# Attention and mixture of experts on one core: v's sums shared by two engines, the router's weights first, the last batch in another order

## The chip, the core and the metric

The program runs on one core of a Trainium2 chip. The core has five engines that run side by side and wait for each other through semaphores: TensorE (PE: matrix products; PEld: its weight loads), VectorE (DVE), ScalarE (ACT), GpSimd (POOL) and SyncE (SP), which here mostly issues transfers. Each engine takes its instructions in order. The metric is the device time of one execution in microseconds (us), as the median of several runs.

## The reference

Eight batches, eight heads, 576 tokens, 64 numbers per head. Keys and values are first averaged over groups of eight tokens, so 576 queries meet 72 keys:

```python
k_p = k.reshape(B, H, Sp, pool, D).mean(axis=3)          # pool = 8
v_p = v.reshape(B, H, Sp, pool, D).mean(axis=3)
scores = scale * np.matmul(q, k_p.transpose(0, 1, 3, 2))
attn = softmax(scores);  x = attn @ v_p                  # x: (4608, 512)
```

Then a router in two steps (the best of 4 groups, then the best of its 4 experts) sends every token to one of 16 experts, and the token's output is its gate times `relu(x @ w1) @ w2` of that expert, with 1024 hidden numbers.

## The kernel before

**Batches.** A batch is 576 tokens: five chunks of 128, 128, 128, 128 and 64. For each batch the attention is computed, the router run, and the expert that most tokens want is applied to the whole batch. The tokens of other experts come afterwards, in blocks of 32 (class `Left`).

**Plans.** The order of the work is written out by hand as strings of pieces: `START`, then `FIRST` for batch 0, `STEADY` for batches 1 to 6, `LAST` for batch 7. A piece such as `a.vr:0:r` calls the method `vr(0, "r")` of the attention of the current batch; `n` and `x` are the attentions of the next two batches, `m` and `w` the expert's work of this batch and the next, `t` the router's weights and dummies, `l` the leftover blocks. Each engine takes its instructions in the order of the plan, transfers included: nearly all are issued by SP, a few by ACT. A transfer into a buffer still in use, or from an address that the kernel has yet to compute, holds SP and all that stands behind it.

**The opening.** `load_k`, `load_v` bring keys and values in two blocks each (512 KB); `load_r` the remainder of 16 rows per head pair: 64 lanes of v (`rem[0:64]`) and 64 of k (`rem[64:128]`). `kr`, `vr` and `rr` add groups of eight by `total` (L211): on VectorE one reduction (`r`), on Pool three additions that halve the row (`p`). `kt` (L263) turns the summed keys on TensorE, and its `tail` the keys' remainder; `kta` copies them. `qt` and `qta` turn and copy a chunk of queries. `sc`, `mx`, `sb`, `ex`, `su_`, `nm`, `pt` are the softmax of a chunk: scores (PE), maximum and subtraction (DVE), exponential (ACT), sums (DVE), normalization (POOL, `:p`), transposition (DVE). `rep` (L239) spreads the summed values to where the attention product `av` wants them; `repa` and `repd` copy them by ACT and VectorE. `ava` and `avd` take the product out.

**The guess.** Batch 0 takes its expert by a guess from the averaged values alone: `guess_x` (L476, 20 small products of all of `vp` and the remainder), one ACT copy, `guess_e` (L486, four products with the router's weights and some small VectorE operations), and SP reads the elected number in `elect` (L472). Only then can SP issue `m.load:1:j`, the expert's weights of 512 KB each. `split` (ACT) and `spd` (VectorE `v` or two Pool subtractions `p`) part each weight block into a high and a low piece. `up` (L567) is a first expert product of 12 passes: `up:f` reads weight block f//2. `ua`, `upd` take it out; `down` (8 passes a piece) and `half` are the second product. `t.load_wr` asks, on ACT's queue, for the router's weights in two transfers; `turn_wr` turns them on TensorE, `put_wr` copies them. `t.warm:z` multiplies ones by ones z times (two passes each), with a result that nobody reads.

**Last batch.** Its plan mixes the expert's work with the leftover blocks: ten `l.step`, `l.which`, fetches, then `whole`, `turn`, `gather`, `up`, `down` of one block. Before, its first product is `m.up:3:0`.

Of the kernel before, what the change touches and what calls it, by code (L numbers as in the profile page):

```python
# [8 lines left out]
F32 = mybir.dt.float32  # L9
# [8 lines left out]
B, H, S, D = 8, 8, 576, 64  # L18
# [16 lines left out]
TCARGS = dict(schedule_with_timeline_sim=True)  # L35

START = """
a.load_k:1:w a.load_k:0:w a.load_q:0 a.qt:0 a.load_r:k a.load_r:v a.load_q:1 a.kr:0:r a.kr:1:p a.load_v:0 a.load_v:1 a.rr:r a.qta:0 a.load_q:3 a.kt
n.load_r:v t.load_wr a.kta a.qt:1 a.load_q:4 a.vr:0:r a.sc:0 a.mx:0 t.turn_wr a.qta:1 a.vr:1:p a.sc:1 a.load_q:2 t.warm:2 a.sb:0 n.load_r:k a.ex:0
n.load_k:0 a.mx:1 t.put_wr a.sb:1 a.su_:0 a.qt:3 a.ex:1 a.rep a.guess_x a.nm:0:p a.su_:1 a.repd:1 a.repa:1 a.nm:1:p n.load_v:1 a.pt:0 a.repa:0 a.qt:2  # L40
a.repd:0 a.qta:3 n.load_k:1 a.pt:1 a.guess_e n.kr:0:r a.av:0:1 a.ava:0:0 a.ava:0:1 a.avd:0:1 a.ava:0:3 a.qt:4 m.load:1:1 m.load:1:2 m.load:1:3
a.ava:0:2 a.qta:2 a.sc:3 a.avd:0:3 a.avd:0:0 m.load:1:0 a.avd:0:2 n.kr:1:p a.mx:3 a.sb:3 m.split:1:1 a.ex:3 n.load_qb:3 m.spd:1:1:v n.load_qb:1 a.sc:2
a.su_:3 t.warm:4 a.nm:3:p a.qta:4 t.warm:7
"""
FIRST = """
m.split:1:3 a.mx:2 m.up:2:0 n.load_qb:2 m.split:1:2 m.ua:2:0 a.sc:4 a.sb:2 t.warm:8 m.spd:1:2:p m.up:3:0 a.pt:3 m.up:4:0 m.up:5:0 a.ex:2 a.mx:4 a.sb:4
# [26 lines left out]
w.load:2:0 x.nm:0:p w.spd:1:0:v w.load:2:1 x.repa:1 m.da:1 m.down:11 w.split:1:1 x.pt:0 m.da:3 n.gates w.load:1:2 w.spd:1:1:p n.keep_x  # L73
"""
LAST = """
m.up:3:0 m.up:2:0 m.up:3:1 m.ua:3:0 m.split:1:3 m.ua:2:0 m.up:1:0 m.up:1:1 m.split:1:2 m.upd:2:0 l.xtiles m.ua:3:1 l.step m.ua:1:0 l.step m.spd:1:2:p
m.ua:1:1 m.up:5:0 m.spd:1:3 m.up:7:0 m.upd:3:0 m.up:4:0 m.upd:3:1 m.ua:5:0 m.ua:4:0 m.load:2:2 m.load:2:3 m.upd:1:0 m.upd:1:1 m.up:0:0 m.up:2:1
m.up:5:1 m.up:6:0 m.ua:7:0 l.step l.step l.step m.ua:2:1 m.ua:0:0 m.upd:5:0 m.up:4:1 m.split:2:1 m.ua:5:1 l.step l.step l.step m.split:2:2 m.ua:6:0
m.upd:4:0 m.up:7:1 m.ua:4:1 l.step m.spd:2:1:p m.split:2:0 l.step l.tiles m.ua:7:1 m.up:0:1 m.spd:2:0:p m.upd:7:0 m.up:6:1 l.which m.upd:0:0 m.upd:2:1
l.fetch_x l.fetch_b:1 m.split:2:3 m.spd:2:3:p m.upd:5:1 m.down:0 m.upd:6:0 l.slots m.ua:6:1 m.upd:4:1 m.upd:7:1 m.spd:2:2:v m.upd:6:1 l.rows l.whole:1  # L80
m.down:1 m.down:3 l.whole:3 l.whole:0 l.whole:2 l.whole:4 l.turn:0 l.fetch_a:1 l.turn:1 l.turn:3 m.ua:0:1 m.down:4 l.turn:2 l.turn:4 l.gather m.down:5
m.upd:0:1 m.da:1 l.next_ l.back m.half:3:1 l.up m.down:6 l.hback l.fetch_a m.down:12 l.fetch_x m.down:2 l.down l.slots m.down:13 m.down:7 m.da:0
m.down:8 l.fetch_b m.da:4 m.da:2 m.half:3:0
"""


# [1 line left out]
def attn_moe(ctx: ExitStack, tc: tile.TileContext, q, k, v, wg, we, w1, w2, out):  # L88
    nc = tc.nc
# [7 lines left out]
    ident = keep.tile([128, 128], F32, name="ident")  # L97
# [10 lines left out]
    for u in range(4):  # L108
        r = slice(32 * u, 32 * u + 32)
# [37 lines left out]
    wk = ctx.enter_context(tc.tile_pool(name="wk", bufs=1))  # L147
    sm = ctx.enter_context(tc.tile_pool(name="sm", bufs=2))
    ps_m = ctx.enter_context(tc.tile_pool(name="ps_m", bufs=3, space=PSUM))
# [9 lines left out]
    class Att:  # L159
# [67 lines left out]
                s.kp = wk.tile([128, NG, D], F32, name="kp")  # L227
            s.total(s.kp[:, 2 * u:2 * u + 2], s.k[u], eng)

        def rr(s, eng="r"):  # L230
            s.rp = wk.tile([128, D], F32, name="rp")
            s.total(s.rp, s.rem, eng)

        def vr(s, u, eng="p"):
            if s.vp is None:
                s.vp = wk.tile([128, 4, D], F32, name="vp")
            s.total(s.vp[:, 2 * u:2 * u + 2, :], s.v[u], eng)

        def rep(s):  # L239

# [20 lines left out]
            tt(out=s.v5[:, o:o + 2 * w].rearrange("p (a b) d -> p a b d", a=2), in0=ps.rearrange("p a (b d) -> p a b d", d=D), in1=ms, op=ALU.mult)  # L261

        def kt(s):  # L263
            tail = lambda ps: [nc.tensor.matmul(ps[64 * a:64 * a + 64, 256:320], lhsT=s.rp[64:128], rhs=ident[64:128, 64:128], start=True, stop=True) for a in range(2)]
            ps = s.tk = ps_t.tile([128, 512], F32, name="tp")
            if s.b:
                for z in range(2):
                    nc.tensor.transpose(out=ps[:, 128 * z:128 * z + 128], in_=flat(s.kp[:, 2 * z:2 * z + 2, :]), identity=ident)
                tail(ps)
                return  # L270
            for g in range(NG):
                for y in range(2):
                    nc.tensor.matmul(ps[64 * y:64 * y + 64, 128 * g:128 * g + 128], lhsT=s.kp[:, 2 * (g % 2) + g // 2], rhs=ident, start=True, stop=True)
            ps = s.tk2 = ps_m.tile([128, 512], F32, name="mm")
            tail(ps)

        def kta(s):
            ps = s.tk
# [682 lines left out]
```

## Time and profile before

| what | value |
|---|---|
| median of 3 runs | 556.96 us (553.56 to 557.68) |
| the profiled execution | 557.65 us |
| its span | 555.9 us |
| PE busy | 529.3 us (95%) |
| DVE, POOL, ACT busy | 360.8, 275.8, 211.7 us |
| chain that ended last | PE 83%, DVE 5%, DMA 5% |

The span is the part of the execution that the trace covers. Busy time of TensorE is modelled, as matrix products overlap. The chain that ended last is followed back from the last instruction, at each step to what released it. In a timeline row the first number is the start in us from the span's start, the second how long it took, `xN` how many instructions it stands for, and brackets give the idle time of the engine before it and what ended it.

### The profile page before, as it was taken

The numbers are of one execution on the slowest core, as the hardware profiler recorded it, in microseconds if no ns is written. First come the engines' busy times: TensorE is split into PE (matmuls) and PEld (weight loads), VectorE is DVE, ScalarE is ACT, GpSimd is POOL, SyncE is SP. The second block draws the span as 40 slices with busy tenths as digits, with TensorE's granted clock in tenths as the row PEclk, the third lists the DMA queues.
The fourth block names the chain that finished last, engine by engine and source line by source line (L and its number), as shares of the span: only waits on it lengthen the run. The fifth ranks groups of instructions, "written<-read, shape, count | busy, mean of one in ns | idle before, by whom it ended". The sixth has DMA issues, their size and how long they took to land.

```text
span 555.9 us, 15235 instructions
## 1 busy us (share of the span) xinstructions
PE 529.3 (95%) x6218; PEld 471.4 (85%) x6218; DVE 360.8 (65%) x940; ACT 211.7 (38%) x402; POOL 275.8 (50%) x259
## 2 busy tenths in 40 slices
PE   3889999999999999999999999999999999999995
PEld 3789988799888998899788998899788987799874
DVE  4678898758756775767656775767657764347420
ACT  2244523445225452454325451454234451335111
POOL 3437386036924577057914686157904644175300
PEclk9999999999999999999999999999999999999998
DMA  9787561590519714591519623693518000725701
GB/s 234 157 198 179 150 126 50 170 334 30 101 42 314 192 46 78 198 284 44 104 50 339 157 64 61 241 381 71 123 62 279 33 2 27 261 102 199 275 31 62
DMA packets 115648, 81.32 MB, mean 146 GB/s; under 512 B 73562, under 2 KB 92250, under 8 KB 115192
## 3 DMA queue, kind: packets, MB, share of 16 engines
q1 hardware_dynamic: 110256, 70.92, 45.7%
q10 hardware_dynamic: 5288, 9.35, 4.5%
q8 instruction: 50, 0.82, 0.7%
q14 instruction: 22, 0.18, 0.1%
q0 software_dynamic: 32, 0.04, 0.0%
HBM read 75.01 MB, written 28.38 MB: 186 GB/s over the span
## 4 chain that ended last, share of the span: by engine, by line
PE 83%; DVE 5%; DMA 5%; ACT 2%; issue 2%; SPq 1%; POOL 1%; ACTq 0%; POOLq 0%
PE mm L578 35%; PE mm L617 26%; PE sc L374 5%; PE mm L622 4%; PE sc L320 4%; DMA sw<-in_moe_w_dram 3%; PE tp L408 1%; DMA rem<-in_k_dram 1%; DMA ht<-in_moe_w_expert_dram 1%; PE mm L597 1%; PE sc L244 1%; PE mm L910 1%; ACT w L555 1%; PE tp L374 1%; DVE pT L355 1%
## 5 line engine op out<-in xcount | busy, mean ns | idle before, releaser
L578 PE MATMUL mm<-xt,w 128*128 128x320 f32 (+1 forms) x1536 | 212.4, 298 | 2.1 <-POOL w L565 1.2
L578 PEld LDWEIGHTS mm<-xt,w 128*128 128x128 f32 x1536 | 205.6, 189 | 5.6 <-POOL w L565 1.6
L617 PE MATMUL mm<-w,ht 128*128 128x512 f32 x744 | 177.4, 393 | 0.0
L565 POOL TENSOR_TENSOR w<-sw,w 128x512 fp32r<-128x512 f32 x94 | 122.8, 1332 | 84.9 <-ACT w L555 74.5
L617 PEld LDWEIGHTS mm<-w,ht 128*128 128x128 f32 x744 | 138.0, 188 | 31.1 <-issue 2.5
L349 POOL TENSOR_TENSOR p<-p,su 128x576 f32<-128x576 f32 (+1 forms) x40 | 45.8, 1150 | 135.7 <-DVE su L344 128.5
L583 ACT ACTIVATE ht<-mm 128x320 fp32r<-128x320 f32 (+1 forms) x128 | 49.6, 408 | 110.6 <-PE mm L578 110.3
L588 DVE SCALAR_TENSOR_TENSOR ht<-mm,ht 128x256 fp32r<-128x256 f32 (+1 forms) x192 | 60.2, 344 | 41.2 <-ACT ht L583 40.1
L555 ACT CAST w<-sw 128x1024 fp32r<-128x1024 f32 x64 | 66.1, 1043 | 19.4 <-DMA sw<-in_moe_w_dram 14.9
L630 ACT ACTIVATE y<-mm,gm 128x512 f32<-128x512 f32 x31 | 21.3, 687 | 67.7 <-PE mm L617 63.5
L399 POOL TENSOR_TENSOR sw<-xt 128x640 f32<-128x640 f32 (+1 forms) x28 | 40.0, 1461 | 7.7 <-DVE xt L392 7.7
L342 DVE TENSOR_REDUCE su<-p 128x8 f32<-128x576 f32 (+1 forms) x40 | 29.7, 743 | 15.1 <-ACT p L337 15.0
L309 DVE STREAM_TRANSPOSE qT<-q 128x512 f32<-128x512 f32 x35 | 24.4, 700 | 20.7 <-PE sc L320 14.9
L218 POOL TENSOR_TENSOR kv<-kv 128x512 f32<-128x512 f32 x21 | 29.0, 1379 | 10.0 <-DMA kv<-in_v_dram 7.7
L326 DVE TENSOR_REDUCE mx<-sc 128x8 f32<-128x576 f32 (+1 forms) x40 | 29.4, 735 | 6.2 <-PE sc L320 6.2
L374 PE MATMUL sc<-pT,v 32*64 32x128 f32 (+11 forms) x1560 | 31.0, 290 | 2.0 <-issue 1.3
L355 DVE STREAM_TRANSPOSE pT<-p 128x576 f32<-128x576 f32 (+1 forms) x40 | 30.8, 769 | 3.1 <-POOL p L349 3.1
L337 ACT ACTIVATE p<-p 128x576 f32<-128x576 f32 (+1 forms) x40 | 27.4, 684 | 13.4 <-DVE p L333 9.9
L622 PE MATMUL mm<-w,ht 128*128 128x512 f32 x128 | 32.4, 396 | 0.0
L374 PEld LDWEIGHTS sc<-pT,v 32*64 32x64 f32 (+3 forms) x1560 | 27.4, 139 | 5.1 <-issue 4.0
L561 DVE TENSOR_TENSOR w<-sw,w 128x1024 fp32r<-128x1024 f32 x17 | 25.1, 1478 | 10.0 <-ACT w L555 10.0
L320 PEld LDWEIGHTS sc<-kT,qT 64*64 64x64 f32 x1264 | 24.1, 142 | 7.4 <-issue 3.0
(217 smaller groups left out, 492.4 us busy)
## 6 DMA issues: line engine op xcount, KB each, us to landing
sw<-in_moe_w_dram SPq DMA_DIRECT2D x72, 512.0 KB
xscr<-xt SPq DMA_DIRECT2D x8, 2304.0 KB
kv<-in_v_dram SPq DMA_DIRECT2D x16, 512.0 KB
q<-in_q_dram SPq DMA_DIRECT2D x112, 72.0 KB
out_dram<-y ACTq DMA_DIRECT2D x31, 256.0 KB
kv<-in_k_dram SPq DMA_DIRECT2D x14, 512.0 KB
kv<-in_moe_w_dram SPq DMA_DIRECT2D x6, 512.0 KB
pT<-xscr SPq DMA_DIRECT2D x2, 1152.0 KB
```

The costliest lines, as they stand in the source:

```text
L320: nc.tensor.matmul(ps[t:t + 64, y, SP * g:SP * g + SP], lhsT=s.qT[c][r, g, w:w + 64], rhs=k, start=True, stop=True)
L349: (nc.vector if eng == "v" else nc.gpsimd).tensor_tensor(out=pf, in0=pf, in1=bc(sf, SP), op=ALU.mult)
L355: nc.vector.transpose(out=s.pT[0:n, :, 32 * c:32 * c + 32], in_=s.p[c].rearrange("p u x s -> p (u x s)").rearrange("p (b i) -> p b i", i=3 ...
L374: nc.tensor.matmul(to[64 * x:64 * x + 64], lhsT=w, rhs=s.pT[e, k, 32 * c0:32 * c0 + n], start=(z == 0), stop=(z == 2))
L399: nc.gpsimd.tensor_tensor(out=x, in0=a, in1=b, op=ALU.add)
L555: nc.scalar.copy(out=wh, in_=raw)
L565: nc.gpsimd.tensor_tensor(out=wl[:, p], in0=raw[:, p], in1=wh[:, p].bitcast(F32), op=ALU.subtract)
L578: nc.tensor.matmul(ps[:, 0:n], lhsT=l[:, kc, fs], rhs=xt[:, r, kc, sl], start=(kc == 0 and i == 0), stop=(kc == 3 and i == 2))
L583: nc.scalar.activation(out=s.ht[f][:, o:o + n], in_=s.pu[f, hf][:, 0:n], func=AF.Relu)
L588: stt(out=ht[:, at:at + hi - lo], in0=ps[:, lo - o:hi - o], scalar=0.0, in1=ht[:, lo:hi].bitcast(F32), op0=ALU.max, op1=ALU.subtract)
L617: nc.tensor.matmul(ps, lhsT=s.ht[f][:, 640 * l + o:640 * l + o + 128], rhs=s.w[2, f // 2][r][:, f % 2, :], start=(i == 0), stop=(i == 23))
L622: nc.tensor.matmul(ps, lhsT=s.ht[f][:, 512:640], rhs=s.w[2, f // 2][r][:, f % 2, :], start=(i == 0), stop=(i == 15))
```

## The change

In the opening `vr` can sum half a block (`t` is 0 or 1), and `rr` one part of the remainder (`v` or `k`). Of each block of v VectorE sums one half and Pool the other; VectorE sums the keys' remainder, Pool v's. The turn of the keys' remainder is a piece of its own, `ktail`. On ACT `t.load_wr` is first. On SP `load_r:v` stands behind `load_q:1` and `load_v:0`, `load_q:4` ahead of `n.load_r:v`, and `n.load_k:1` behind the four `m.load`. On TensorE `turn_wr` follows the second scores, `guess_x` precedes `qt:3` and `rep`, `qt:2` follows `guess_e`; of the dummies two stand at the start and one ahead of `guess_x`, and the two pieces at the end of `START` are 4 and 4 where they were 4 and 7. `LAST` has the same pieces in another order. `FIRST` and `STEADY` are as they were.

```diff
@@ -35,12 +35,12 @@
 START = """
-a.load_k:1:w a.load_k:0:w a.load_q:0 a.qt:0 a.load_r:k a.load_r:v a.load_q:1 a.kr:0:r a.kr:1:p a.load_v:0 a.load_v:1 a.rr:r a.qta:0 a.load_q:3 a.kt
-n.load_r:v t.load_wr a.kta a.qt:1 a.load_q:4 a.vr:0:r a.sc:0 a.mx:0 t.turn_wr a.qta:1 a.vr:1:p a.sc:1 a.load_q:2 t.warm:2 a.sb:0 n.load_r:k a.ex:0
-n.load_k:0 a.mx:1 t.put_wr a.sb:1 a.su_:0 a.qt:3 a.ex:1 a.rep a.guess_x a.nm:0:p a.su_:1 a.repd:1 a.repa:1 a.nm:1:p n.load_v:1 a.pt:0 a.repa:0 a.qt:2
-a.repd:0 a.qta:3 n.load_k:1 a.pt:1 a.guess_e n.kr:0:r a.av:0:1 a.ava:0:0 a.ava:0:1 a.avd:0:1 a.ava:0:3 a.qt:4 m.load:1:1 m.load:1:2 m.load:1:3
-a.ava:0:2 a.qta:2 a.sc:3 a.avd:0:3 a.avd:0:0 m.load:1:0 a.avd:0:2 n.kr:1:p a.mx:3 a.sb:3 m.split:1:1 a.ex:3 n.load_qb:3 m.spd:1:1:v n.load_qb:1 a.sc:2
-a.su_:3 t.warm:4 a.nm:3:p a.qta:4 t.warm:7
+t.load_wr t.warm:2 a.load_k:1:w a.load_k:0:w a.load_q:0 a.load_r:k a.load_q:1 a.qt:0 a.kr:0:r a.kr:1:p a.load_v:0 a.load_r:v a.load_v:1 a.qta:0
+a.load_q:3 a.kt a.rr:r:k a.ktail a.kta a.qt:1 a.load_q:4 a.vr:0:r:0 a.vr:0:p:1 a.rr:p:v n.load_r:v a.qta:1 a.sc:0 a.mx:0 a.sc:1 a.sb:0 t.turn_wr
+a.vr:1:r:0 a.vr:1:p:1 a.ex:0 a.mx:1 a.load_q:2 t.put_wr n.load_r:k n.load_k:0 a.sb:1 a.ex:1 t.warm:1 a.guess_x a.su_:0 n.load_v:1 a.nm:0:p a.su_:1
+a.qt:3 a.rep a.nm:1:p a.repd:1 a.pt:0 a.guess_e a.repa:1 a.repa:0 a.repd:0 a.qta:3 a.qt:2 m.load:1:1 m.load:1:2 m.load:1:3 m.load:1:0 a.pt:1
+n.load_k:1 n.kr:0:r a.av:0:1 a.qt:4 a.ava:0:0 a.ava:0:1 a.avd:0:1 a.ava:0:3 a.ava:0:2 a.qta:2 a.avd:0:3 a.avd:0:0 a.avd:0:2 a.sc:3 n.kr:1:p
+m.split:1:1 m.spd:1:1:v a.mx:3 a.sb:3 a.ex:3 n.load_qb:3 n.load_qb:1 a.sc:2 a.su_:3 t.warm:4 a.nm:3:p a.qta:4 t.warm:4
 """
...
 LAST = """
-m.up:3:0 m.up:2:0 m.up:3:1 m.ua:3:0 m.split:1:3 m.ua:2:0 m.up:1:0 m.up:1:1 m.split:1:2 m.upd:2:0 l.xtiles m.ua:3:1 l.step m.ua:1:0 l.step m.spd:1:2:p
-m.ua:1:1 m.up:5:0 m.spd:1:3 m.up:7:0 m.upd:3:0 m.up:4:0 m.upd:3:1 m.ua:5:0 m.ua:4:0 m.load:2:2 m.load:2:3 m.upd:1:0 m.upd:1:1 m.up:0:0 m.up:2:1
-m.up:5:1 m.up:6:0 m.ua:7:0 l.step l.step l.step m.ua:2:1 m.ua:0:0 m.upd:5:0 m.up:4:1 m.split:2:1 m.ua:5:1 l.step l.step l.step m.split:2:2 m.ua:6:0
...
+m.up:0:0 m.up:1:0 m.up:3:0 m.ua:0:0 m.up:3:1 l.xtiles m.ua:3:0 m.up:2:0 m.split:1:2 m.upd:0:0 l.step m.spd:1:2:p m.ua:2:0 m.ua:1:0 l.step m.up:0:1
+m.up:5:0 m.load:2:2 m.up:1:1 m.upd:3:0 m.upd:2:0 m.ua:3:1 m.upd:1:0 m.upd:3:1 l.step m.up:4:0 l.step m.up:2:1 m.ua:0:1 l.step m.upd:0:1 l.step
+m.split:1:3 m.ua:5:0 m.upd:5:0 m.split:2:1 m.ua:1:1 m.load:2:3 l.step l.step m.upd:1:1 l.step l.step m.spd:1:3 l.tiles m.ua:4:0 m.up:5:1 m.up:7:0
+l.which m.ua:2:1 m.ua:5:1 m.split:2:2 l.fetch_x m.up:6:0 m.upd:4:0 l.fetch_b:1 m.split:2:0 m.ua:6:0 m.up:4:1 m.upd:2:1 m.up:6:1 m.spd:2:0:p l.slots
+m.upd:5:1 m.ua:7:0 m.ua:4:1 m.ua:6:1 m.upd:7:0 m.upd:4:1 m.upd:6:0 m.split:2:3 m.spd:2:1:p m.upd:6:1 l.rows m.spd:2:2:v l.whole:1 l.whole:3 m.down:3
+l.whole:0 l.whole:2 m.up:7:1 l.whole:4 m.down:4 m.ua:7:1 l.turn:0 l.fetch_a:1 l.turn:1 l.turn:3 m.down:12 m.spd:2:3:p l.turn:2 l.turn:4 l.gather
+m.upd:7:1 l.next_ m.half:3:1 m.down:13 l.back m.da:4 m.down:0 l.up m.down:1 l.hback l.fetch_a m.down:2 l.fetch_x m.down:5 l.down m.down:6 m.down:7
+l.slots m.da:1 l.fetch_b m.da:0 m.down:8 m.da:2 m.half:3:0
 """
...
@@ -227,14 +227,19 @@
                 s.kp = wk.tile([128, NG, D], F32, name="kp")
             s.total(s.kp[:, 2 * u:2 * u + 2], s.k[u], eng)
 
-        def rr(s, eng="r"):
-            s.rp = wk.tile([128, D], F32, name="rp")
-            s.total(s.rp, s.rem, eng)
-
-        def vr(s, u, eng="p"):
+        def rr(s, eng="r", part=None):
+            if s.rp is None:
+                s.rp = wk.tile([128, D], F32, name="rp")
+            r = {None: slice(0, 128), "v": slice(0, 64), "k": slice(64, 128)}[part]
+            s.total(s.rp[r], s.rem[r], eng)
+
+        def vr(s, u, eng="p", t=None):
             if s.vp is None:
                 s.vp = wk.tile([128, 4, D], F32, name="vp")
-            s.total(s.vp[:, 2 * u:2 * u + 2, :], s.v[u], eng)
+            if t is None:
+                s.total(s.vp[:, 2 * u:2 * u + 2, :], s.v[u], eng)
+            else:
+                s.total(s.vp[:, 2 * u + t, :], s.v[u][:, t], eng)
 
         def rep(s):
 
@@ -261,18 +266,21 @@
             tt(out=s.v5[:, o:o + 2 * w].rearrange("p (a b) d -> p a b d", a=2), in0=ps.rearrange("p a (b d) -> p a b d", d=D), in1=ms, op=ALU.mult)
 
         def kt(s):
-            tail = lambda ps: [nc.tensor.matmul(ps[64 * a:64 * a + 64, 256:320], lhsT=s.rp[64:128], rhs=ident[64:128, 64:128], start=True, stop=True) for a in range(2)]
             ps = s.tk = ps_t.tile([128, 512], F32, name="tp")
             if s.b:
                 for z in range(2):
                     nc.tensor.transpose(out=ps[:, 128 * z:128 * z + 128], in_=flat(s.kp[:, 2 * z:2 * z + 2, :]), identity=ident)
-                tail(ps)
+                s.ktail(ps)
                 return
             for g in range(NG):
                 for y in range(2):
                     nc.tensor.matmul(ps[64 * y:64 * y + 64, 128 * g:128 * g + 128], lhsT=s.kp[:, 2 * (g % 2) + g // 2], rhs=ident, start=True, stop=True)
-            ps = s.tk2 = ps_m.tile([128, 512], F32, name="mm")
-            tail(ps)
+
+        def ktail(s, ps=None):
+            if ps is None:
+                ps = s.tk2 = ps_m.tile([128, 512], F32, name="mm")
+            for a in range(2):
+                nc.tensor.matmul(ps[64 * a:64 * a + 64, 256:320], lhsT=s.rp[64:128], rhs=ident[64:128, 64:128], start=True, stop=True)
 
         def kta(s):
             ps = s.tk
```

## Rows read from the trace of the kernel before

**Rows 1.** Stretches: us, busy us of each engine (instructions), granted clock, DMA share, GB/s.

```profile
10.00:20.00 10.00, 7.15 (x94) 5.60 (x90) 6.34 (x7) 2.99 (x7) 2.44 (x3) 1.00 1.10 239
...
480.00:490.00 10.00, 8.36 (x49) 6.95 (x48) 2.94 (x14) 4.38 (x7) 5.63 (x4) 1.00 1.04 371
```

**Rows 2.** Chain of waits, in order of time: start, us, what.

```profile
19.06 0.85 PE mm L298 x4
...
19.91 1.17 PE sc L244 x8
...
21.39 2.51 PE tp L482 x20
...
46.18 2.53 PE sc L374 x116
```

**Rows 3.** Timeline of the opening, up to v's sums: start, us, engine, line, operation.

```profile
10.34 1.01 DVE L215 TENSOR_REDUCE rp<-rem 128x64 f32<-128x512 f32 x1 [2.37 <-DMA rem<-in_v_dram]
...
12.58 1.92 DVE L215 TENSOR_REDUCE vp<-kv 128x128 f32<-128x1024 f32 x1 [1.23 <-DMA kv<-in_v_dram]
...
15.03 1.26 POOL L218 TENSOR_TENSOR kv<-kv 128x512 f32<-128x512 f32 x1 [7.68 <-DMA kv<-in_v_dram]
...
16.10 0.64 PE L900 MATMUL mm<-ident,ht 20*128 20x20 f32 x4 [2.00 <-DMA ht<-in_moe_w_expert_dram]
...
16.37 0.72 POOL L219 TENSOR_TENSOR kv<-kv 128x256 f32<-128x256 f32 x1
...
17.17 0.46 POOL L223 TENSOR_TENSOR vp<-kv 128x128 f32<-128x128 f32 x1
```

**Rows 4.** Timeline, the guess and the first weight request.

```profile
24.72 1.73 PE L490 MATMUL tp<-wr,ht 128*128 128x20 f32 x8
...
27.56 0.15 DVE L471 TENSOR_SCALAR me<-ct 128x1 int32<-128x1 f32 x1
...
28.76 2.49 SPq L548 DMA_DIRECT2D sw<-in_moe_w_dram  x4
```

**Rows 5.** Timeline, the next keys, the weights' landings and the fourth chunk.

```profile
25.81 1.27 POOL L218 TENSOR_TENSOR kv<-kv 128x512 f32<-128x512 f32 x1 [2.34 <-DMA kv<-in_k_dram]
...
32.49 1.05 ACT L555 CAST w<-sw 128x1024 fp32r<-128x1024 f32 x1 [0.93 <-DMA sw<-in_moe_w_dram]
...
36.51 2.00 ACT L555 CAST w<-sw 128x1024 fp32r<-128x1024 f32 x2 [0.54 <-DMA sw<-in_moe_w_dram]
...
37.31 1.15 POOL L349 TENSOR_TENSOR p<-p,su 128x576 f32<-128x576 f32 x1 [8.87 <-DVE su L344]
...
38.50 0.77 DVE L355 STREAM_TRANSPOSE pT<-p 128x576 f32<-128x576 f32 x1
...
39.84 0.75 DVE L326 TENSOR_REDUCE mx<-sc 64x8 f32<-64x576 f32 x1 [0.57 <-PE sc L320]
```

**Rows 6.** Timeline, TensorE's dummy passes.

```profile
17.84 1.22 PE L910 MATMUL mm<-ones 128*128 128x128 f32 x4
...
34.22 3.50 PE L910 MATMUL mm<-ones 128*128 128x128 f32 x22
...
39.73 2.05 PE L910 MATMUL mm<-ones 128*128 128x128 f32 x16
```

**Rows 7.** Timeline, start of the last batch.

```profile
479.62 1.23 DVE L561 TENSOR_TENSOR w<-sw,w 128x1024 fp32r<-128x1024 f32 x1 [3.42 <-ACT w L555]
...
484.34 0.39 PE L578 MATMUL mm<-xt,w 128*128 128x256 f32 x1 [0.42 <-ACT w L555]
...
484.37 2.50 POOL L565 TENSOR_TENSOR w<-sw,w 128x512 fp32r<-128x512 f32 x2 [19.19 <-ACT w L555]
...
485.69 0.98 PE L578 MATMUL mm<-xt,w 128*128 128x256 f32 x6 [0.96 <-POOL w L565]
...
486.92 7.26 PE L578 MATMUL mm<-xt,w 128*128 128x256 f32 x53 [0.26 <-POOL w L565]
...
491.24 5.05 POOL L565 TENSOR_TENSOR w<-sw,w 128x512 fp32r<-128x512 f32 x4
```

More of the change, by code (lines that the diff above doesn't have):

```diff
@@ L75 @@
 LAST = """
-m.up:3:0 m.up:2:0 m.up:3:1 m.ua:3:0 m.split:1:3 m.ua:2:0 m.up:1:0 m.up:1:1 m.split:1:2 m.upd:2:0 l.xtiles m.ua:3:1 l.step m.ua:1:0 l.step m.spd:1:2:p
-m.ua:1:1 m.up:5:0 m.spd:1:3 m.up:7:0 m.upd:3:0 m.up:4:0 m.upd:3:1 m.ua:5:0 m.ua:4:0 m.load:2:2 m.load:2:3 m.upd:1:0 m.upd:1:1 m.up:0:0 m.up:2:1
-m.up:5:1 m.up:6:0 m.ua:7:0 l.step l.step l.step m.ua:2:1 m.ua:0:0 m.upd:5:0 m.up:4:1 m.split:2:1 m.ua:5:1 l.step l.step l.step m.split:2:2 m.ua:6:0
[L79 to L83, printed above, removed]
+m.up:0:0 m.up:1:0 m.up:3:0 m.ua:0:0 m.up:3:1 l.xtiles m.ua:3:0 m.up:2:0 m.split:1:2 m.upd:0:0 l.step m.spd:1:2:p m.ua:2:0 m.ua:1:0 l.step m.up:0:1
[6 more added lines that the diff above has]
+l.slots m.da:1 l.fetch_b m.da:0 m.down:8 m.da:2 m.half:3:0
 """
```

## The prediction

> **What bounds the kernel now.** The page's engine table comes first: TensorE is the engine that is busy nearly all the time, so what the change does elsewhere counts only if it moves TensorE's work or fills its holes. The table by stretches says where the holes are: TensorE is busy 7.15 of the 10 us between 10 and 20, and 8.36 of the 10 us between 480 and 490; after that the page's slices show it full until it has finished [rows 1]. The chain of waits says who sets the opening: after the early loads it runs through TensorE's own queue (queries turned, `rep`, `guess_x`), and at 39.84 it leaves TensorE for VectorE's maximum of the fifth chunk, from which it comes back at 46.18 with the second attention product [rows 2, 5]. From there TensorE is full for tens of us, so a shift at 46.18 is a shift of the end. In the last batch the chain is simply TensorE, behind a stall at its start [rows 7].
>
> The profiled execution took 557.65 us, 1.75 us more than its 555.9 us span; it stands 0.69 us above the median of 556.96. The sum is made against 557.65 and carried over to the median.
>
> **Opening, up to the guess.** Before, TensorE waits 2.00 us for the router's weights, which ACT asked for late; the turn of them stands ahead of the second scores [rows 3]. The change puts the two requests first on ACT's queue, past the first query copy. They cost ACT issue time while it has nothing else to do, and the turn also moves behind the second scores. That wait goes. What is late next is v's sums: `guess_x` now stands directly behind them on TensorE.
>
> Their price. The keys' remainder is a reduction over 64 partitions instead of 128: same length per lane, so the 1.01 of its row, but it no longer waits for v's remainder [rows 3]. v's first half drops on VectorE from 1.92 to about 1.01, the row of a 128x512 source. Pool gets three pieces of 128x512 or 64x512, each three additions: 0.72 and 0.46 from rows, the third not shown; below the 0.46 and above nothing, I take 0.3, since each halving took away less than the one before. With gaps 1.65 us a piece [rows 3]. Pool starts with the first half of v, at 12.58, and finishes three pieces at 17.5; before it finished v at 17.17 + 0.46 = 17.63 [rows 3]. VectorE's second piece is done by 16.2 (15.03 + 1.01 and little wait). So splitting v in itself buys 0.1 us; both engines were idle there, 7.68 us on Pool, so the six added additions cost nothing.
>
> The gain is the order. `guess_x` took 2.51 us at 21.39, behind one query turn (0.85) and `rep` (1.48) [rows 2]. Now it starts on the first three pieces and waits for the last: three tenths of it are then done, so it ends near 19.3. The query turn and `rep` follow, `guess_e` starts at 21.6 instead of 24.72, and with the row's own distance to the election (27.56 - 24.72) and from there to the first weight request (28.76), the request leaves at 25.65, 3.1 us earlier [rows 4]. If TensorE waits for the whole of v's tile instead, this is 0.7 later; that end is kept.
>
> **What the early guess collides with.** `n.load_k:1` used to be issued before the guess and landed at 25.81, when Pool took it up [rows 5]. Now it is one request behind four weight requests of 512 KB on SP's queue, and SP cannot issue it before the election. `load_r:v`, moved behind a query and a v request, is wanted by Pool only after its first piece. `n.load_r:v` waits for the buffer that Pool's second piece now frees near 15.9, where VectorE freed it at 11.35 [rows 3]; behind it on SP stand a query, the keys' remainder, `n.load_k:0` and `n.load_v:1`, all wanted after 23, so I cost that at nothing; without that room the next keys' sum on VectorE would be late by the 4.5 us. How late does `n.load_k:1` land? The first weight block landed 3.73 after its request and the third 7.75 after [rows 4, 5], so two blocks cost 4.02. The fourth block and the keys come after it: at the 371 GB/s of a stretch with a full queue 1.41 us each [rows 1], at the 2.01 just read 2.01 each. That gives 25.65 + 7.75 + 2.8 to 4.0 = 36.2 to 37.4. I take 36.4, near the full rate, since nothing of small packets stands between.
>
> Behind it on Pool wait `n.kr:1` itself (1.26 + 0.72 + 0.46 and gaps, 2.55), `nm:3` (1.15), and behind that on VectorE the transposition `pt:3` (0.77) and then the maximum of the fifth chunk [rows 3, 5]. `nm:3` ran at 37.31; now it can't before 38.95. So the maximum starts at 36.4 + 2.55 + 1.15 + 0.77 + 0.06 = 40.93, where it was 39.84: the early guess ends in **1.1 us lost**. Pool's split `spd:1:2` follows `nm:3` and is done near 42.7, when TensorE wants it.
>
> TensorE itself would arrive earlier: the fill of dummy products in front of the first expert product has 16 passes for 22, 6 x 0.128 = 0.77 by the fast row, and up to 0.5 comes from the earlier first attention product [rows 6]. That 1.1 us is spent waiting at the second attention product. The two extra dummies at the start and the one before `guess_x` lie in time in which TensorE waits for data.
>
> **The clock.** The granted clock reads 1.00, the 2.4 GHz level, in every stretch, the first included [rows 1]; but the same dummy pass takes 1.22/4 = 0.305 us at 17.84 and 2.05/16 = 0.128 at 39.73, and the 22 passes at 34.22 take 3.50, so somewhat over 1 us of them runs at the early pace [rows 6]. The Trainium skill ("TensorE: Matmul & The Clock Gate", Part 1) calls the slow state the default, which activity releases; by that the shorter fill could leave TensorE slow for longer, where the column shows no change at all. This is a rival below.
>
> **Last batch.** TensorE idles 0.42 + 0.96 + 0.26 = 1.64 us at its start, since `up:3:0` is first and wants the low part of weight block 1, which Pool ends at 486.87 [rows 7]. The low part of block 0 was made by VectorE at 479.62 + 1.23 = 480.85. The change starts with `up:0:0` and `up:1:0`, both on block 0: 24 passes, at the 7.26/53 = 0.137 of the last of these rows 3.3 us, so TensorE reaches block 1 near 487.2, when it is ready [rows 7]. The stall goes: **1.64 us gained**. The rest has the same products in another order. Block 2 is wanted after six products, 483.92 + 6 x 1.64 = 493.8 at the earliest (the counting products come on top), and Pool, which came to it at 491.24 before, makes it by 493.75 [rows 7]; block 3 is wanted five products later, for as much Pool work. `up:7:1` moves behind the first down product; what it feeds (the chunks from 256 on) is also later. I cost this at nothing because TensorE's queue is never without another ready product; without that cover each late split costs its 2.5 us, the row of two Pool subtractions [rows 7].
>
> **Sum:** +1.1 - 1.64 = -0.5, 557.1 against the profiled 557.65, or **556.4** against the median.
>
> **The rivals.**
> *The keys land in time.* If `n.load_k:1` lands by 34.2, Pool and VectorE are ready when TensorE is, and the opening gains its 1.1: -1.1 - 1.64 = -2.7, 554.2. For it: VectorE waited 0.57 us for TensorE at 39.84 before [rows 5]. Against it: 2 MB of weights ahead at any rate seen.
> *The keys land later: slower than before.* Same place, price one for one: from a landing at 37.0 on the whole change loses. With the 2.01 per block and the guess 0.5 later it is 37.9: 1.5 more than forecast, +1.0, 557.9.
> *The clock rises later.* Then all 16 passes take 0.305, 4.9 us for about 2.8, and the first expert product after them (12 passes of 0.137 at the fast pace, 1.64) takes about double, an estimate; the fifth scores come near 43, VectorE's maximum 3.3 late, and +3.3 - 1.64 = +1.7, 558.6. The Trainium skill's rule on the clock gate is the ground for it; by the granted clock's column it can't be. The rows at 17.84 side with the rule, but the scores that directly precede the fill are unchanged, and before it rose soon after them.
> *The last batch only moves its hole.* The gain is eaten by a late split or a bank not free: +1.1, 558.1.
>
> **How the numbers follow.** Forecast 0.38, keys in time 0.17, keys later 0.18, clock 0.09, last batch 0.08, and 0.10 for something that I don't see, half of it on either side. The centres run from 554.2 to 558.6. The three runs before span 553.56 to 557.68, so a median of the new kernel can fall 1 us to either side of its case: the range is 553.2 to 559.6. The forecast's own part is 555 to 557.8. What a measurement can tell from no change is about 1%, 5.6 us; no case reaches that, so within it 0.90, and the unseen gives faster 0.05 and slower 0.05.
>
> **What would show it.** Right: the first weight request near 25.7; Pool idle before `n.kr:1`, waiting for the key load, to 36 or later; VectorE idle before `pt:3` on Pool, and TensorE pausing about 1 us before the second attention product near 47; no pause of TensorE after the first expert products of the last batch. Wrong: `n.kr:1` on Pool before 34; dummy passes still at 0.3 us at the end of the fill; new pauses of TensorE after 490, above all before `up:5:0` or the whole-batch turns; or a later router request, if TensorE still waits for it ahead of the second scores.

## The result, and the profile after

| what | before | changed |
|---|---|---|
| median of 20 runs each | 555.88 us (553.24 to 559.91) | 559.3 us (556.74 to 562.3) |
| ratio to before | | 1.006, 95% interval 1.0043 to 1.0077 |
| profiled execution, span | 557.65, 555.9 us | 562.3, 560.6 us |

The change costs 3.4 us. That is under the 1% that was called no change, but clear of zero and on the other side of the forecast of 0.5 us gained. The profiled execution of the changed kernel is the slowest of its runs, so its trace shows the loss somewhat large. Ratios, here and below, use the fast runs alone; two of the six runs of e4 (567.95 and 568.08 us) were slow, and the time given for e4 is the median of the other four.

Where it went is read by following TensorE. The second attention product, which started at 46.18 [rows 2], starts at 52.08: 5.9 us late. The 40 passes of the second product behind which the last batch starts begin at 481.68, where the same row of before is at 474.69: 7.0 late. TensorE ends its last product at 553.87 and ended it at 549.21: 4.7 late. So 5.9 us are lost up to the second attention product, 1.1 more on the way to the last batch (0.5 of them in that product itself, 3.03 for 2.53), and the last batch gives 2.3 back. The last two of these readings are in the timelines of TensorE, before:

```profile
474.69 9.23 PE L617 MATMUL mm<-w,ht 128*128 128x512 f32 x40
...
546.18 3.03 PE L597 MATMUL mm<-w,ht 128*128 128x256 f32 x24
```

and changed:

```profile
481.68 9.23 PE L625 MATMUL mm<-w,ht 128*128 128x512 f32 x40
...
550.84 3.03 PE L605 MATMUL mm<-w,ht 128*128 128x256 f32 x24
```

**The opening up to the weights went nearly as forecast.** Timeline of the changed kernel, its steps up to the first weight request (start, us, engine, line, operation; in brackets the idle time before it and what ended it). Lines behind the last edit are 8 higher than before, so L910 is now L918.

```profile
13.08 0.73 POOL L218 TENSOR_TENSOR kv<-kv 128x256 f32<-128x256 f32 x1 [5.48 <-DMA kv<-in_v_dram]
...
14.42 0.32 POOL L223 TENSOR_TENSOR vp<-kv 128x64 f32<-128x64 f32 x1
...
14.80 0.67 PE L908 MATMUL mm<-ident,ht 20*128 20x20 f32 x4
...
17.64 0.32 POOL L223 TENSOR_TENSOR vp<-kv 128x64 f32<-128x64 f32 x1
...
18.01 0.37 PE L490 MATMUL tp<-selg,vp 128*64 128x4 f32 x2 [1.08 <-POOL vp L223]
...
22.38 1.90 PE L498 MATMUL tp<-wr,ht 128*128 128x20 f32 x8
...
25.36 0.15 DVE L479 TENSOR_SCALAR me<-ct 128x1 int32<-128x1 f32 x1
...
26.56 2.11 SPq L556 DMA_DIRECT2D sw<-in_moe_w_dram  x4
...
28.79 0.67 SPq L176 DMA_DIRECT2D kv<-in_k_dram  x1
```

The wait for the router's weights is gone. Pool's third addition took 0.32 (0.3 was estimated), v was whole at 17.96, and the first weight request left at 26.56 instead of 28.76 [rows 4]: 2.2 us earlier.

**Then the keys are late.** Timeline of the changed kernel, Pool, VectorE and TensorE from 37 us on.

```profile
37.30 1.67 PE L586 MATMUL mm<-xt,w 128*128 128x256 f32 x12
...
40.26 1.27 POOL L218 TENSOR_TENSOR kv<-kv 128x512 f32<-128x512 f32 x1 [18.35 <-DMA kv<-in_k_dram]
...
42.85 1.15 POOL L357 TENSOR_TENSOR p<-p,su 128x576 f32<-128x576 f32 x1
43.95 2.51 POOL L573 TENSOR_TENSOR w<-sw,w 128x512 fp32r<-128x512 f32 x2
...
44.03 0.78 DVE L363 STREAM_TRANSPOSE pT<-p 128x576 f32<-128x576 f32 x1 [4.97 <-POOL p L357]
44.73 0.71 DVE L334 TENSOR_REDUCE mx<-sc 64x8 f32<-64x576 f32 x1
...
45.27 0.98 PE L586 MATMUL mm<-xt,w 128*128 128x256 f32 x6 [2.13 <-POOL w L573]
...
46.52 1.43 PE L586 MATMUL mm<-xt,w 128*128 128x256 f32 x5 [0.27 <-POOL w L573]
...
49.22 2.93 PE L586 MATMUL mm<-xt,w 128*128 128x256 f32 x12 [1.26 <-DVE ht L596]
...
52.08 3.03 PE L382 MATMUL sc<-pT,v 32*64 32x96 f32 x192
```

Pool sat idle for 18.35 us and took up the next batch's keys only at 40.26. Everything behind that on Pool follows at once: the normalization (before at 37.31 [rows 5]) at 42.85, the split of a weight block at 43.95. TensorE pauses 2.13 us for that split, then 0.27, then 1.26 for VectorE, whose release of an expert product stands in its queue behind the late transposition.

Stretches of the changed kernel: us, busy us of PE, PEld, DVE, ACT and POOL (instructions), granted clock, DMA share, GB/s.

```profile
10.00:20.00 10.00, 8.75 (x109) 7.33 (x108) 7.82 (x12) 3.04 (x8) 5.20 (x10) 1.00 0.79 185
36.00:38.00 2.00, 2.00 (x19) 2.00 (x19) 1.49 (x4) 2.00 (x4) 0.00 (x0) 1.00 0.83 89
38.00:40.00 2.00, 2.00 (x29) 1.79 (x28) 1.02 (x2) 1.52 (x3) 0.00 (x0) 1.00 0.34 52
46.00:47.00 1.00, 0.73 (x5) 0.53 (x4) 0.96 (x3) 0.68 (x1) 0.46 (x1) 0.70 0.85 136
47.00:53.00 6.00, 4.74 (x65) 4.22 (x65) 4.85 (x11) 0.82 (x4) 2.29 (x2) 0.50 0.15 25
490.00:500.00 10.00, 9.96 (x77) 9.59 (x76) 1.92 (x6) 4.72 (x10) 8.65 (x8) 1.00 0.76 274
```

TensorE is busy 1.6 us more between 10 and 20 than in [rows 1], with the wait gone, and 9.96 of 10 us at the start of the last batch, where it was 8.36. New is the middle: behind the first of these pauses the granted clock falls (0.70 from 46 to 47) to 0.50, the 1.2 GHz level, for over six us, and the 12 passes at 49.22 take 2.93 where 12 passes at 37.30 took 1.67.

**The last batch** starts without a hole; the same two rows of the changed kernel as in [rows 7]:

```profile
490.74 7.67 PE L586 MATMUL mm<-xt,w 128*128 128x256 f32 x60
498.46 0.44 PE L700 MATMUL sc<-loh,both 128*128 128x384 f32 x1
```

The row of before that answers to the second:

```profile
494.03 0.34 PE L692 MATMUL sc<-loh,both 128*128 128x384 f32 x1
```

Before, from the end of the product ahead (484.34 - 0.42) to this row it took 10.11 us; now 7.72.

### The profile page after: what moved, and what is told of

The parts are those of the page before. It is cut to its first block, busy times and chain, and to the rows that moved or that the text cites. A ratio compares the mean times of both kernels' runs of the same rounds, so it can differ in the third digit from the quotient of the medians.

```text
span 560.6 us, 15229 instructions
## 1 busy us (share of the span) xinstructions
PE 532.4 (95%) x6214; PEld 473.3 (84%) x6214; DVE 358.9 (64%) x941; ACT 211.8 (38%) x402; POOL 277.9 (50%) x265
## 5 line engine op out<-in xcount | busy, mean ns | idle before, releaser
L586 PE MATMUL mm<-xt,w 128*128 128x256 f32 (+1 forms) x1536 | 214.3, 299 | 4.8 <-POOL w L573 2.4
L218 POOL TENSOR_TENSOR kv<-kv 128x512 f32<-128x512 f32 (+1 forms) x22 | 30.2, 1371 | 23.8 <-DMA kv<-in_k_dram 18.3
L382 PE MATMUL sc<-pT,v 32*64 32x128 f32 (+10 forms) x1560 | 31.7, 293 | 3.8 <-issue 1.9
L400 DVE TENSOR_TENSOR xt<-sc,xt 128x480 fp32r<-128x480 f32 (+3 forms) x36 | 21.3, 617 | 15.7 <-ACT xt L396 15.5
```

Source lines behind the costliest of these rows:

```text
L218: add(out=a[..., 0:256], in0=a[..., 0:256], in1=a[..., 256:512], op=ALU.add)
L382: nc.tensor.matmul(to[64 * x:64 * x + 64], lhsT=w, rhs=s.pT[e, k, 32 * c0:32 * c0 + n], start=(z == 0), stop=(z == 2))
L586: nc.tensor.matmul(ps[:, 0:n], lhsT=l[:, kc, fs], rhs=xt[:, r, kc, sl], start=(kc == 0 and i == 0), stop=(kc == 3 and i == 2))
```

## The experiments

The theory after the result: the loss is the late load of the next batch's keys, passed on by Pool's queue; the last batch gains. The rivals: the new opening is slow for something else in it (the split sums, the shorter fill, the clock), or the late keys hurt by their transfers and not by Pool's order. Ratios are to the kernel before on the same chip, with their 95% intervals.

### The last batch alone, and the opening alone

```diff
 e1: the kernel before, LAST of the changed kernel
 e2: the changed kernel, LAST of the kernel before
```

> The kernel before with the new order of the last batch alone. Theory (the late key load costs in the opening, the last batch gains): TensorE reaches the last batch at the time of before, its 1.64 us stall is gone, and the end comes 1.6 to 2.3 us earlier: 553.6 to 554.3 where the kernel before has 555.9. Rival (the last batch is what costs, or it only moves its hole): 555.9 or more.

> The new opening with the old order of the last batch. Theory: the whole loss is here, and without the last batch's gain it is larger than that of the change: 560.5 to 562 where the kernel before has 555.9; n.kr:1 starts on Pool at 39 or later. Rival (the last batch costs, the opening is neutral): 555 to 556.5.

Measured: e1 553.49 us, 0.9927 (0.9889 to 0.9965); e2 563.25 us, 1.0134 (1.0101 to 1.0167). Run again later beside the last three experiments, e1 gave 552.96 us, 0.9939 (0.9924 to 0.9955):

> The kernel before with only the last batch's new order, run again on the chip of the three others, so that old and new opening can be compared on one chip. If the new opening costs what the earlier runs suggest, it lies 0.2 to 0.5% below the new opening with early keys; if it costs nothing, level with it.

So the parts have opposite signs: the opening costs 1.3%, some 7.5 us, and the last batch gains 0.6 to 0.7%, 3.4 to 4.1 us. The second run of e1 shows the gain in its trace, 60 passes without a break at the start of the last batch:

```profile
482.67 7.67 PE L578 MATMUL mm<-xt,w 128*128 128x256 f32 x60
```

### The keys' load moved back, and moved alone

```diff
 e3: the changed kernel
-... a.guess_x a.su_:0 n.load_v:1 a.nm:0:p ... m.load:1:0 a.pt:1
-n.load_k:1 n.kr:0:r ...
+... a.guess_x a.su_:0 n.load_v:1 n.load_k:1 a.nm:0:p ... m.load:1:0 a.pt:1
+n.kr:0:r ...
 e4: the kernel before
-a.repd:0 a.qta:3 n.load_k:1 a.pt:1 a.guess_e ... m.load:1:0 a.avd:2
+a.repd:0 a.qta:3 a.pt:1 a.guess_e ... m.load:1:0 n.load_k:1 a.avd:2
```

> The changed kernel with n.load_k:1 issued ahead of the guess again, all else as changed. Theory: the keys land near 24, Pool sums them before 30, no pause of TensorE at 43, the granted clock stays at 1.00, and the second attention product starts at 45.5 to 46.2; with the last batch's gain 553 to 554.3 (before: 555.9, changed: 559.3). Rival (the split sums, the earlier guess or the shorter fill cost by themselves): 557 or more, with a pause of TensorE between 37 and 50 that does not go back to Pool waiting for keys.

> The kernel before with n.load_k:1 alone moved behind the four weight requests. Theory: the keys land 11 to 14 us after the first weight request at 28.8, so at 40 to 42.5; the second attention product starts at 50 or later, TensorE pauses before the third first-product and the granted clock falls: 560 to 564. Rival (the order of that one load costs nothing, the loss is elsewhere in the opening): 555 to 557.

Measured: e3 555.73 us, 0.9981 (0.9956 to 1.0006); e4 564.9 us, 1.0129 (1.0077 to 1.018). Timeline of e3, the keys' first addition on Pool and the second attention product:

```profile
26.48 1.27 POOL L218 TENSOR_TENSOR kv<-kv 128x512 f32<-128x512 f32 x1 [4.58 <-DMA kv<-in_k_dram]
...
45.41 2.53 PE L382 MATMUL sc<-pT,v 32*64 32x96 f32 x192
```

Timeline of e4, the same, with TensorE's pauses between:

```profile
39.49 1.28 POOL L218 TENSOR_TENSOR kv<-kv 128x512 f32<-128x512 f32 x1 [16.23 <-DMA kv<-in_k_dram]
...
44.49 2.71 PE L578 MATMUL mm<-xt,w 128*128 128x256 f32 x11 [3.48 <-POOL w L565]
...
48.44 2.93 PE L578 MATMUL mm<-xt,w 128*128 128x256 f32 x12 [1.23 <-DVE ht L588]
...
51.29 3.47 PE L374 MATMUL sc<-pT,v 32*64 32x96 f32 x192
```

Putting the one request back takes 0.8% from the changed kernel, 4.4 us; moving it alone in the kernel before costs what the whole new opening costs, with pauses for the same two engines in the same order. The cause is shown from both sides. But e3 stays above e1, which has the old opening and the same last batch: not all of the opening's loss is the keys.

### Pool's order

```diff
 e5: the changed kernel
-... a.avd:0:2 a.sc:3 n.kr:1:p
+... a.avd:0:2 a.sc:3
-... t.warm:8 m.spd:1:2:p m.up:3:0
+... t.warm:8 m.spd:1:2:p n.kr:1:p m.up:3:0
```

> The changed kernel with one step moved: the rotation's first sum of the next batch's keys, n.kr:1 on Pool, stands behind m.spd:1:2 instead of ahead of nm:3; the keys' transfer is as late as before. Theory (the late keys cost time only because Pool's in-order queue stands behind them): nm:3 and m.spd:1:2 run near 37 to 39 us, TensorE's pause of 2.13 us in front of the MLP's up passes is gone, the second attention product starts near 46 to 47.5 us instead of 52.08, and the time is 554.5 to 557 us. Rival (late keys and weights harm by what their transfers do to each other, not by Pool's order): the product starts at 50 us or later and the time stays near 559 us.

Measured: 555.6 us, 0.9976 (0.9951 to 1.0001), as forecast by the theory. The timeline of e5, Pool and the second attention product:

```profile
38.48 1.15 POOL L357 TENSOR_TENSOR p<-p,su 128x576 f32<-128x576 f32 x1 [16.49 <-DVE su L352]
39.59 2.51 POOL L573 TENSOR_TENSOR w<-sw,w 128x512 fp32r<-128x512 f32 x2
42.06 1.27 POOL L218 TENSOR_TENSOR kv<-kv 128x512 f32<-128x512 f32 x1
...
47.78 2.53 PE L382 MATMUL sc<-pT,v 32*64 32x96 f32 x192 [0.36 <-DVE pT L363]
```

The keys' request is where the change put it, and 4.7 us are back, as many as with the early request. So the keys themselves are not needed so soon; what hurt was that two pieces which TensorE does need, the normalization and the split, stood behind them on Pool.

### Are the keys late because of small packets?

```diff
 e6: the changed kernel, load_qb of batch 1, head groups 1 and 3
-q[s.b, 4 * y + g].rearrange("(j t) (e d) -> e t j d", t=32, e=2)[e]
+q[s.b, 4 * y + g].rearrange("(e t j) (c d) -> e t (j c) d", e=2, t=32, d=32)[e]
```

> The changed kernel with the next batch's queries of head groups 1 and 3 read as contiguous rows of 2304 bytes instead of pieces of a few hundred bytes; it leaves out the right order of those queries. Theory (the keys, put behind the weights, land late because the queries' small packets share the queues with their last pieces): n.kr:1 starts on Pool at 36.4 to 37.5 us instead of 40.26 and the time is near 556 us. Rival (the keys are late by their own place behind four weight pieces): n.kr:1 still starts at 38.5 us or later, and the time stays near 559 us.

Measured: 558.84 us, 1.0051 (1.0022 to 1.0081), no different from the changed kernel. Pool took the keys up at 38.16; but e2 and e7, with the queries as they were and the same opening, took them up at 37.95 and 38.62. The rival stands: the keys are late by their place. The theory of the small packets is not borne out: from 32 to 36 us only 59 of the 1082 packets of e6 were under 512 B, where in the changed kernel 898 of 1897 were, and the keys came between those of e2 and e7.

The trace of e6 is worth reading for another thing. Its keys came as late as those of e2, and TensorE's long pause was alike, but here the clock held. Timeline of e6, two rows of TensorE:

```profile
47.10 1.69 PE L591 MATMUL mm<-xt,w 128*128 128x256 f32 x12 [1.83 <-DVE ht L601]
...
48.90 2.52 PE L387 MATMUL sc<-pT,v 32*64 32x96 f32 x192
```

One stretch of e6 (the granted clock is the third number from the end):

```profile
48.00:50.00 2.00, 1.89 (x97) 1.68 (x101) 1.93 (x3) 1.18 (x3) 0.04 (x1) 1.00 0.00 0
```

The same two rows in the timeline of e2:

```profile
46.91 2.73 PE L586 MATMUL mm<-xt,w 128*128 128x256 f32 x12 [1.80 <-DVE ht L596]
...
49.58 2.97 PE L382 MATMUL sc<-pT,v 32*64 32x96 f32 x192
```

And the same stretch of e2:

```profile
48.00:50.00 2.00, 2.00 (x36) 1.77 (x39) 1.59 (x2) 0.32 (x2) 0.00 (x0) 0.50 0.00 0
```

At 0.50 these two rows take 1.04 + 0.45 = 1.5 us longer. That is what the clock adds to the pause in the runs in which it falls.

### Dummy passes in the pauses

```diff
 e7: the changed kernel
-... m.spd:1:2:p m.up:3:0 a.pt:3 m.up:4:0 m.up:5:0
+... m.spd:1:2:p m.up:3:0 t.warm:8 a.pt:3 m.up:4:0 t.warm:3 m.up:5:0
```

> The changed kernel, keys as late as before, with eight dummy passes of TensorE behind the first up product that waits (m.up:3:0) and three behind m.up:4:0, in the stretch where it pauses for 2.13 us and where the granted clock then falls to 0.50. Theory (part of the 5.9 us by which the second attention product is late is the clock that falls with the pause, 12 passes of up taking 2.93 us for 1.67): the clock stays at 1.00 between 46 and 54 us, 1.5 to 3 us come back, 556.3 to 558 us. Rival (the pause itself is all, the low clock costs nothing on the path or falls as before): 559 to 560 us.

Measured: 564.19 us, 1.0132 (1.011 to 1.0153): slower, which neither expected. Timeline of e7:

```profile
47.66 2.37 PE L586 MATMUL mm<-xt,w 128*128 128x256 f32 x12 [1.92 <-DVE ht L596]
...
61.29 4.33 PE L586 MATMUL mm<-xt,w 128*128 128x256 f32 x20 [4.32 <-issue]
```

The dummies write the same tile `mm` as the expert products. The product behind them now waits for VectorE's release, where in the changed kernel the one at 45.27 waited for Pool; that the dummies took its place in the ring of these tiles is the likely reason, but no run shows it. The clock fell all the same (0.58 between 48 and 50 us). And TensorE stood for 4.32 us later, by the section below for its next instructions. As a measure of the clock this run tells nothing; the pair above does.

### What is left: the fill and the rest of the opening

```diff
 e8: e3, last fill of START      t.warm:4 -> t.warm:7   (22 passes)
 e9: e1, last fill of START      t.warm:7 -> t.warm:4   (16 passes)
 e10: e8, ahead of a.guess_x     t.warm:1 -> t.warm:6
 e11: e1, ahead of t.turn_wr     t.warm:5 added
```

> The changed kernel with the next batch's keys asked for ahead of the guess (as in the experiment that gave 555.73 us) and the last fill of TensorE put back from 16 passes to 22. Theory (the two microseconds that the new opening still costs with early keys come from the shorter fill, by a granted clock that is lower between 35 and 50 us in some executions): about 553.5 us, clock 1.00 from 40 us. Rival (they come from elsewhere in the new opening): 555.7 us or more, the longer fill adding up to 0.9 us where TensorE would otherwise go on.

> The kernel before with the last batch's new order (553.49 us) and, of the new opening, only the shorter last fill: 16 passes for 22. Theory (the shorter fill is what costs): 555 to 556 us, with a clock under 1.00 somewhere between 40 and 50 us. Rival (the fill's length does not matter where the keys are early): 552.5 to 553.8 us.

> The kernel with early keys and the fill of 22 passes (554.28 us before), with five more dummy passes ahead of the guess's first products, where TensorE pauses for 1.1 to 2.7 us in all of the runs of the new opening and where the granted clock falls to 0.50 in most of them. Theory (what the new opening still costs beside the old one is this low clock): the clock holds 1.00 from 18 us on, the second attention product starts before 46.5 us, and the time is 0.2 to 0.5% below that of the run without them, level with the old opening with the new last batch. Rival (the low clock there costs nothing, for the passes between 18 and 30 us took as long at 0.50 as at 1.00): no change, 0.9952 of the kernel before.

> The old opening with the last batch's new order (553.49 us), with five dummy passes in the 2.0 us pause ahead of the turn of the router's weights, where the granted clock fell in its profiled run. Theory (a clock that falls there costs the runs in which it falls): 552 to 553 us, a narrower spread. Rival (it costs nothing): level with the same kernel without the passes.

Measured: e8 554.28 us, 0.9952 (0.993 to 0.9973); e9 553.92 us, 0.9955 (0.993 to 0.9981); e10 554.35 us, 0.9966 (0.9942 to 0.9991); e11 553.02 us, 0.9939 (0.9922 to 0.9955).

- **The fill.** From 22 to 16 passes goes 0.9952 to 0.9981 with the new opening, 0.29%. With the old one it goes 0.9927 to 0.9955, 0.28%, or, with the second run of e1, 0.9939 to 0.9955, 0.16%: 0.9 to 1.6 us. All pairs are measured on different chips, each difference lies inside its intervals, e9 stands close to its rival (553.8), and its clock held 1.00. So a price of the fill is possible and not shown.
- **The rest of the opening.** New against old at equal fill: 0.9952 to 0.9927 (0.9939 by e12), 0.9981 to 0.9955, and on one chip 0.9966 (e10) to 0.9939 (e12): 0.13 to 0.27%, 0.7 to 1.5 us, again each inside its intervals.
- **What the pace before 35 us costs was not measured.** e10 expected 0.2 to 0.5% from holding the clock; it fell at 20 us all the same, and the time is that of e8. The clock's column of e12 reads 1.00 there, but its trace holds no record of the clock ahead of 35.76, and its turn of queries (four passes) took 1.11 us at 23.77, the slow pace; in e11 it took 0.66 at 21.68, and the clock fell to 0.50 at 23. So of these two e11 is the faster up to 23 us.
- **An earlier guess alone bought nothing that shows.** The first weight request left at 26.67 in the profiled run of e11 and at 28.82 in that of e12, 2.15 us later, and the times of the two are level.

e10 did bring the guess forward: its first attention product started at 25.09 where the changed kernel's did at 26.69. The trace of e10 shows where it went, in a pause that has no releaser ("issue"):

```profile
19.11 0.66 PE L306 MATMUL mm<-ident,q 128*128 128x128 f32 x4
...
22.51 1.09 PE L306 MATMUL mm<-ident,q 128*128 128x128 f32 x4
25.09 3.18 PE L382 MATMUL sc<-pT,v 32*64 32x64 f32 x188 [1.48 <-DVE pT L363]
30.77 0.48 PE L382 MATMUL sc<-pT,v 24*64 24x64 f32 x4 [2.50 <-issue]
```

Such idle time of TensorE between 27 and 34 us, 0.37 to 2.50, stands in six of the eight traces with the new opening (0.40 in the changed kernel), and in one of six with the old (0.84 in e11): 0.7 us on average against 0.1, so it may be part of what is left.

What TensorE waits for there can be read from the packets. One DMA queue carries instructions in packets of 16 KB; the page of before lists it as

```profile
q8 instruction: 50, 0.82, 0.7%
```

(packets, MB, share). In e10 such a packet ended at 29.54 and TensorE went on at 30.77; in e7 at 59.82 and 61.29, the end of the 4.32 us; in the changed kernel at 31.51 and 32.80. All 67 idle times of TensorE's products that the timelines of the 14 traces mark "issue", 0.17 to 4.32 us long, end 1.2 to 1.6 us behind the end of such a packet, and there are only 50 of these in a trace of some 556 us. So, as far as the traces tell, TensorE stands in these pauses for its next instructions; no run changes that load. What makes the packet late in one execution and not in another no run shows.

## Why the prediction was wrong

**The step that failed** is the landing of `n.load_k:1`, put at 36.4, which is 10.75 us behind the first weight request, with 36.2 to 37.4 around it. Pool took the keys up at 40.26 in the profiled run, at 37.95 to 39.49 in e2, e4, e6 and e7. Of the 3.9 us between 36.4 and 40.26, 0.9 is the request, which left at 26.56 for 25.65. The rest is the transfer: 13.7 us from the first weight request to Pool's start here, 11.6 in e2, 11.8 in e6, 12.0 in e7, 12.7 in e4. The near end of the range was taken because "nothing of small packets stands between"; the far end (11.8 behind the request) fits e2 and e6. The volume was right: from 28 to 36 us the queues moved 296 to 353 GB/s, about 2.6 MB, which is as much as the five requests of 512 KB. But the last pieces were not among it: from 36 to 40 us it was 89 and 52 GB/s. Packets of the changed kernel from 32 to 36 and from 36 to 40 us:

```profile
DMA packets 1897, 1.35 MB, mean 338 GB/s; under 512 B 898, under 2 KB 1681, under 8 KB 1897
...
DMA packets 1458, 0.28 MB, mean 70 GB/s; under 512 B 1416, under 2 KB 1416, under 8 KB 1456
```

The weights came in packets of 1 KB, the last of which ended at 35.89. The keys' 256 packets of 2 KB are those between the counts for 2 and for 8 KB: 216 in the first stretch, 40 in the second, beside the packets of the 16 requests for queries, issued from 30.55 on. The queue's mean rate was taken as the rate of the request that stands last in it, while these shared the queues. That such sharing is what holds the keys back is a reading of these stretches; wider query packets did not change it. The changed kernel's trace has one thing more: the last three of the 256 packets start from 38.83 on, where a packet of 16 KB of instructions that began at 37.64 ends (38.84). In e2, e6 and e7 the last keys had ended by 36.88, 37.46 and 37.56, without such a gap. That would be part of the spread from 37.95 to 40.26; no run varies it.

**The chain behind it held to 0.1 us.** From the landing to the fifth chunk's maximum 4.53 us were forecast; it took 44.73 - 40.26 = 4.47. From that maximum to the second product it had taken 46.18 - 39.84 = 6.34; in e6, whose clock held, it took 6.29, in the changed kernel 7.35. So the second product follows the landing by 10.74 us in e6, and by 11.63 (e2), 11.80 (e4) and 11.82 (the changed kernel) where the clock fell. Each us of landing is a us of time, and the rival "the keys land later" was the right mechanism. Its own landing of 37.9 was still early for all but e2.

**What the sum left out** is the clock. The pauses of 2.13, 0.27 and 1.26 us are how TensorE spends the delay, and no cost beside it: e6 had pauses of 0.63, 0.26 and 1.83 and lost nothing between the maximum and the product. But only a clock that rises later was a rival; here it fell to 0.50 in the middle, and 1.0 us more went there up to the second product, another 0.5 in the product. With that the changed kernel's trace adds up: 1.1 forecast, 0.9 for the later request, 2.9 for the transfer and 1.0 for the clock are the 5.9 us. The Trainium skill ("TensorE: Matmul & The Clock Gate", Part 1) calls the throttled state the default that activity releases; the changed kernel agrees, at 0.50 from 47 to 53 behind its pauses, but e6, with a pause of 1.83 us, kept 1.00. The rival named from that page priced the rise at the fill, by 3.3 us; the shorter fill cost at most about 1.6. Where the prediction reads 1.00 for the first stretches, the trace of before holds no record of the clock ahead of 35.88: the slow dummy passes, not the column, told the pace.

**The guess** came 2.2 us earlier, not 3.1: `guess_x` ended at 19.9 for 19.3, since v was whole 0.5 later than forecast, and `guess_e` started at 22.38 for 21.6. No use was made of it: the first attention product, which was to bring up to 0.5 us, started at 26.69, before at 26.74, now behind VectorE's transposition, which stands in its queue behind the election.

**The last batch** was under-sized. The stall of 1.64 us went, as forecast, and nothing came in its place: no wait of TensorE is in the trace of the changed kernel behind 490. From the start of the 40 passes ahead of the last batch to TensorE's last product it takes 74.5 us in the old order (before, e4) and 72.2 in all eleven traces of the new one, 2.3 less. Of these, 0.7 is the passes themselves: all 192 first products of the last batch took 26.8 us before and 26.1 in e12, in which none stands behind a pause. And in the third trace of the old order, e2, it takes 76.0: there the clock fell to 0.50 behind the holes, and the 53 passes which took 7.26 us before took 8.72. The row of e2:

```profile
490.99 8.72 PE L586 MATMUL mm<-xt,w 128*128 128x256 f32 x53 [0.27 <-POOL w L573]
```

So the new order gains 2.3 us, or 3.8 where the holes had cost the clock too; the 3.4 us of the runs (2.5 to 4.2 in e12's interval) lies between. How often the clock falls there no run tells.

**Sum as measured:** the opening about +7 (4.4 to 4.7 by the keys' place ahead of Pool's other work, the rest not told apart: perhaps the fill, and TensorE's waits for instructions), the last batch -3.4; forecast were +1.1 and -1.64. Both signs were right, and the larger one was six times too small. That 559.3 still lies within the stated 553.2 to 559.6 is luck: the opening lost some 6 us more than forecast, the last batch gained 1.8 more, and the two errors partly cancel. The best version here is the kernel before with the last batch's new order: 0.9939, beating the kernel before by 0.6% and the changed one by 1.2%.

## What to carry to other kernels

When a request is moved behind others, price its landing by the queue's tail and not by bytes over the mean rate, and take as the price what waits behind its consumer on that engine, in order: moving that consumer (e5) repaired as much as moving the load back (e3). A pause of TensorE can have a second price, the clock of the work behind it (1.5 us in the opening, 1.5 in e2's last batch), and pauses alike had it in one run and not in another. And time a change's parts apart: here one part gained 3.4 us and the other lost 7.

## What was not expected of the hardware

- The clock's column reads 1.00 where the trace holds no record of the clock, and no trace here has one ahead of 11 us; before, the changed kernel, e7, e9 and e12 have none ahead of 35.7. Where there is a record, the pace agrees with it: the turn of queries of four passes took 0.66 us at 19.11 of e10 under 1.00 and 1.09 at 22.51 under 0.50. Without one, at 19.87 of the changed kernel, it took 1.11 under a column of 1.00. There the length of a known pass tells the pace, not the column.
- Idle time of TensorE that has no releaser follows packets of 16 KB of instructions, in 67 of 67 cases of 0.17 to 4.32 us.
- With the same opening Pool took the keys up at 37.95, 38.62 and 40.26 us in three executions: the tail of a shared queue varies by 2 us.
